# One PSUM bank a product in layer 2's input product, and raw weights stored in the step that joins them

## Chip, core and metric

The kernel runs on one core of a Trainium2 chip. The metric is the device time of one execution in microseconds (us). The core's engines run from queues of their own and wait for each other by semaphores: PE (TensorE, matrix products), DVE (VectorE), ACT (ScalarE), POOL (GpSimd) and SP, which issues the DMAs.

## The reference

Attention between 8 x 8 blocks of 512 tokens and 32 states, then two feed-forward layers. In float32:

```python
scores = scale * np.matmul(x, state.transpose(0, 1, 3, 2))       # 512 x 32 a head, softmax, then
xread = np.matmul(a, state)
sread = np.matmul(a2, x)                                         # a2: softmax of the transposed scores
x = concat([xread, sread])                                       # (8 * 544, 512)
gate = 1.0 / (1.0 + np.exp(-(x @ w_gate)))                       # layer 1, d_ff 1536
x = gate * (x @ w_val) @ w_out
h = x @ w_in                                                     # layer 2, d_ff 2048
g = np.where(h >= 1, h, np.where(h <= -1, 0.0, (h + 1) ** 2 / 4))
out = g @ w_out
```

## The kernel before

Each float32 product is made of three fast ones: both sides are split into a high and a low part (ACT copies the high part, DVE or POOL subtracts for the low one), and high x high, high x low and low x high are added in PSUM. The stages follow each other: attention and layer 1's gated product for the first four batches (`gated(0)`), its output product (`output1(0)`) mixed with the attention of the other four, `gated(1)`, `output1(1)`, layer 2's input product (`unit`, `unit_s`) and layer 2's output product (`second`). The order of the instructions on each engine is the order in which the code writes them.

**Layer 2's input product.** It is a two-by-two block product with seven products in place of eight (M1 to M7). Five blocks (0, 1, 2, "s", 3) follow each other, twice: a number is a pair of batches, "s" the states of all batches. A pair's block has four units, one for each 256 columns of weights; a unit runs the seven products in the order `PO` = M1, M6, M5, M7, M2, M3, M4, each of six matmuls of 512 columns, and calls `tick(n)` after each, where planned other work is written: loads and sums of the next block's operands (`load_y`, tiles `yr`, sums on POOL), their splits (`split_y`, tiles `yc`: high on ACT, low on POOL), the sums and splits of the second layer's output weights (`combos_w2`, tile `w2c`, on DVE and ACT), and stores of results (`puts`). M2 adds to the bank of M1, M3 to that of M5, M4 to that of M7. The unit takes its four banks as two tiles of two banks each from the pools `ps0` and `ps1` that all earlier stages use too:

```python
pa_, pb_ = ps_tile(0), ps_tile(1)
pm = {M1: pa_[:, 0], M6: pa_[:, 1], M5: pb_[:, 0], M7: pb_[:, 1]}
pm |= {M2: pm[M1], M4: pm[M7], M3: pm[M5]}
```

After M1, ACT copies its bank to `m1` (L977 of before); after M6, M5 and M7, DVE adds the bank to `m1` or `sg` (L947); then `act_g2` makes the activation: ACT's relu and square (L930, L931), which use a bank as scratch space, and DVE's clip (L932, the calls of `fins`). The last of a unit's activations are written after the next unit's first and second product (`later`).

**Raw weights.** In `output1(0)` the class `Weights` also converts the weights. One call of `slot` is a step: `high` takes the oldest joined tile, `join` (DVE, L166 and L172) makes the next tile `ca` from two halves, `parts` (ACT, L159 and L160) makes the halves of the one after, `load` loads another (`wraw`), and `flush` issues what is in `stores`. `ca` has three buffers. Weights of the kind "raw" (layer 2's output weights) are not split here: `high` only puts their store to `w2_dram` into `stores`, so it is issued in the step after the one that joined them.

Of the kernel before, what the change touches and what calls it, by code (L numbers as in the profile page):

```python
# [8 lines left out]
F32 = mybir.dt.float32  # L9
# [3 lines left out]
AF = mybir.ActivationFunctionType  # L13
ALU = mybir.AluOpType
AX = mybir.AxisListType
PSUM = bass.MemoryType.PSUM
# [9 lines left out]
def attention_moe_moe_kernel(  # L26
# [28 lines left out]
    nc = tc.nc  # L55
# [11 lines left out]
    NSB = B * N  # L67
# [4 lines left out]
    def pool(name, side="left", bufs=1, stack=None, **kw):  # L72
        return (stack or ctx).enter_context(
            tc.tile_pool(name=name, bufs=bufs, side=side, reuse_waits="tile", **kw)
        )

    st_ps = ExitStack()
# [4 lines left out]
    def ps_tile(k):  # L82
        return psets[k].tile([128, 2, 512], F32, tag="ps", name=f"ps{k}")
# [3 lines left out]
    half = work.tile([128, 1], F32, tag="half", name="half")  # L87
# [38 lines left out]
    def f32(ap):  # L126
        return ap.bitcast(F32)
# [5 lines left out]
    class Weights:  # L133
# [29 lines left out]
        def join(self):  # L163
            if self.first:
                r, a, y, dst = self.first.pop(0)
                nc.vector.scalar_tensor_tensor(  # L166
                    out=y, in0=r[:, 1::2], scalar=0x80000000, in1=y,
                    op0=ALU.bitwise_and, op1=ALU.bitwise_or,
                )
                part = getattr(dst, "kind", None) == "part"  # L170
                o, then = dst() if part else (a, None)
                nc.vector.scalar_tensor_tensor(  # L172
                    out=o, in0=a, scalar=3, in1=y,
                    op0=ALU.logical_shift_left, op1=ALU.bitwise_or,
                )
                if part:
                    then()
                else:
                    self.mid.append((a, dst))

        def high(self):
            if self.mid and getattr(self.mid[0][1], "kind", None) not in closed:
                a, dst = self.mid.pop(0)
                if getattr(dst, "kind", None) == "raw":
                    stores.append(lambda: nc.sync.dma_start(out=dst(), in_=f32(a)))
                    return
                hi, lo, then = dst()
                if len(hi.shape) == 3:
                    a = a.rearrange("p (k f) -> p k f", k=hi.shape[1])
                nc.scalar.activation(out=hi, in_=f32(a), func=AF.Copy)  # L190
                self.second.append((hi, lo, a, then))
# [24 lines left out]
    stores = []  # L216
# [5 lines left out]
    def mm3(ps, terms):  # L222
        n = len(terms)
        for i, (wh, wl, vh, vl) in enumerate(terms):
            nc.tensor.matmul(out=ps, lhsT=wh, rhs=vh, start=(i == 0), stop=False)
            nc.tensor.matmul(out=ps, lhsT=wh, rhs=vl, start=False, stop=False)
            nc.tensor.matmul(out=ps, lhsT=wl, rhs=vh, start=False, stop=(i == n - 1))
# [490 lines left out]
    M1, M2, M3, M4, M5, M6, M7 = range(7)  # L718
# [78 lines left out]
    def combos_w2(i):  # L797
# [27 lines left out]
        def store():  # L825
# [5 lines left out]
            load,  # L831
            [sum_(M5, M7, M1), sum_(M7, M3, M7), sum_(M6, M3, M5), sum_(M4, M2, M6)],
            high,
            [low(n) for n in (0, 2, 4, 6)],
            store,
# [91 lines left out]
    def act_g2(o, s, c):  # L927


        nc.scalar.activation(out=s, in_=c, func=AF.Relu, bias=half, scale=0.5)  # L930
        nc.scalar.activation(out=s, in_=s, func=AF.Square)  # L931
        return lambda: nc.vector.scalar_tensor_tensor(  # L932
            out=o, in0=s, scalar=1.0, in1=c, op0=ALU.min, op1=ALU.max
        )

    def store_g2(j, m, sg):
        return lambda: nc.sync.dma_start(out=hd_dram[j][:, 2 * m : 2 * m + 2], in_=sg)
# [3 lines left out]
    def late(n):  # L941
        while later and (n is None or later[0][0] <= n):
            later.pop(0)[1]()

    def unit(bp, m, tick):
        def add(o, a, b):
            nc.vector.tensor_tensor(out=o, in0=a, in1=b, op=ADD)  # L947

        w = w_t[m]
        pa_, pb_ = ps_tile(0), ps_tile(1)  # L950
        pm = {M1: pa_[:, 0], M6: pa_[:, 1], M5: pb_[:, 0], M7: pb_[:, 1]}
        pm |= {M2: pm[M1], M4: pm[M7], M3: pm[M5]}
        m1 = tmp.tile([128, 512], F32, tag="m1", name="m1", bufs=2)
        sg, fins = [None, None], {}

        def sg_tile(e):
            sg[e] = tmp.tile([128, 2, 512], F32, tag="sg", name="sg", bufs=4)

        def put(e):
            puts.append(store_g2(2 * bp + e, m, sg[e]))  # L960

        for n, j in enumerate(PO):
            y = yc_t[bp, j].rearrange("p l (k f) -> p l k f", k=2)
            more = j in (M2, M4, M3)
            for k in range(2):
                wh, wl = (w[:, l, WI[j], 128 * k : 128 * k + 128] for l in range(2))
                vh, vl = y[:, 0, k], y[:, 1, k]
                for i, (a, b) in enumerate(((wh, vh), (wh, vl), (wl, vh))):
                    nc.tensor.matmul(  # L969
                        out=pm[j], lhsT=a, rhs=b,  # L970
                        start=not more and k == 0 and i == 0,
                        stop=k == 1 and i == 2,
                        skip_group_check=more,
                    )
            late(n)
            if j == M1:
                nc.scalar.activation(out=m1, in_=pm[j], func=AF.Copy)  # L977
            elif j == M6:
                add(m1, pm[j], m1)
            elif j == M5:  # L980
                sg_tile(1)
                add(sg[1][:, 1], pm[j], m1)
            elif j == M7:
                add(sg[1][:, 1], pm[j], sg[1][:, 1])
            elif j == M2:
                sg_tile(0)
                fins[3] = act_g2(sg[1][:, 1], pm[M6], sg[1][:, 1])
            elif j == M3:
                s = spool.tile([128, 512], F32, tag="s", name="s", bufs=2)
                fins[0] = act_g2(sg[0][:, 0], s, pm[M1])  # L990
                fins[3]()
                add(sg[1][:, 0], pm[j], m1)
            elif j == M4:
                fins[0]()
                add(sg[0][:, 1], pm[j], m1)
                fins[1] = act_g2(sg[1][:, 0], pm[M5], sg[1][:, 0])
            tick(n)

        def last():
            fins[2] = act_g2(sg[0][:, 1], pm[M7], sg[0][:, 1])  # L1000
            fins[1]()
            put(1)

        later.append((0, last))
        later.append((1, lambda: (fins[2](), put(0))))

    def unit_s(m, tick):
        w = w_t[m]
        ps = ps_tile(0)[:, :, :NSB]
        bt = st_t["raw_c"].rearrange("p l (k f) -> p l k f", k=4)  # L1010
        dt = st_t["d_c"].rearrange("p l (k f) -> p l k f", k=4)
        for e in range(2):
            terms = ((M5, bt, 0), (M4, dt, 0)) if e else ((M1, bt, 0), (M2, bt, 2))
            mm3(
                ps[:, e],
                [
                    tuple(w[:, l, WI[j], 128 * k : 128 * k + 128] for l in range(2))
                    + (y[:, 0, o + k], y[:, 1, o + k])
                    for j, y, o in terms
                    for k in range(2)  # L1020
                ],
            )
            if e == 0:
                tick(0)
        late(None)
        sg = tmp.tile([128, 2, NSB], F32, tag="sg", name="sg", bufs=4)
        nc.scalar.activation(out=sg, in_=ps, func=AF.Relu, bias=half, scale=0.5)
        nc.scalar.activation(out=sg, in_=sg, func=AF.Square)
        nc.vector.scalar_tensor_tensor(
            out=sg, in0=sg, scalar=1.0, in1=ps, op0=ALU.min, op1=ALU.max  # L1030
        )
        tick(1)
        puts.append(store_g2(B, m, sg))

# [472 lines left out]


    st_o, st_m, st_c, st_x = ExitStack(), ExitStack(), ExitStack(), ExitStack()
    pm_ = pool("ycm", stack=st_m)  # L1510
    y_pools.update({i: pm_ for i in range(3, 10)})
    spool = pool("spool", stack=st_m)
# [101 lines left out]
    for p, b in blocks:  # L1614
        for mi in range(4):

            def tick(n):
                nonlocal t
                if puts and (b == "s" or n in (2, 4)):
                    puts.pop(0)()  # L1620
                for f in at.pop(t, ()):
                    f()
                t += 1
# [13 lines left out]

    st_m.close()
    st_e.close()
    st_ps.close()  # L1640
    hcps.append(pool("hcp1", stack=st_o))
    w2p = pool("w2b", stack=st_o, bufs=4)
    psp = pool("pso", stack=st_o, space=PSUM)
# [35 lines left out]
```

## Time and profile before

| | |
|---|---|
| median of 3 runs | 1749.75 us (1743.32 to 1749.83) |
| the profiled execution's own time | 1750.84 us |
| its span in the trace | 1749.1 us |
| PE busy | 1509.6 us, 86% |
| DVE, ACT, POOL busy | 972.7, 784.1, 225.8 us |
| matmuls of the input product (L969) | 1344, 389.9 us busy, 169.7 us idle before them |

Busy time is the time in which an engine has an instruction in work; a matmul that overlaps the next counts once. "Idle before" is the time an engine stood before the instructions of a group, and behind the arrow stands whose end released it. The times of the table's last rows and of all rows below are from one execution.

### The profile page before, as it was taken

Reading aid. Unit: us, or ns where it says so; the run is one execution under the profiler, and the core shown is the slowest. Engines: PE = TensorE matmul, PEld = TensorE weight load, DVE = VectorE, ACT = ScalarE, POOL = GpSimd, SP = SyncE. Lnnn points to the kernel's source line nnn. Section 1 sums busy time; section 2 is a strip of 40 time slices with the busy share of each in tenths; the row PEclk is TensorE's granted clock in tenths of the full one; section 3 lists DMA queues with packets and bytes.
Section 4 is the critical chain, followed back from the end, with each engine's and each line's share of the span. In section 5 each row is a group of like instructions: output and inputs, shape, how many; then the busy total and the mean of one; then the engine's idle time right before and its main releaser. Section 6 shows DMA issues by size and latency. Waiting matters only on the chain.

```text
span 1749.1 us, 29156 instructions
## 1 busy us (share of the span) xinstructions
PE 1509.6 (86%) x11984; PEld 1257.5 (72%) x11984; DVE 972.7 (56%) x1386; ACT 784.1 (45%) x1156; POOL 225.8 (13%) x108
## 2 busy tenths in 40 slices
PE   7999977899999999997776776767677799999997
PEld 6677756787677877985554564555555689999997
DVE  5766565644666266345343443444454468778775
ACT  6655365534654254233544445344354334443442
POOL 3000030000000000002332434234151000000000
PEclk9999999999999999999898988898889899999999
DMA  6245478745665499663233445523415674434432
GB/s 193 98 160 179 161 234 299 245 147 181 242 251 214 146 329 376 244 224 109 102 121 138 151 161 188 212 104 123 163 51 189 220 276 138 133 121 134 133 121 85
DMA packets 146453, 310.19 MB, mean 177 GB/s; under 512 B 15504, under 2 KB 82064, under 8 KB 143248
## 3 DMA queue, kind: packets, MB, share of 16 engines
q1 hardware_dynamic: 146056, 308.06, 50.4%
q8 instruction: 94, 1.54, 0.4%
q14 instruction: 39, 0.32, 0.1%
q10 hardware_dynamic: 264, 0.26, 0.1%
HBM read 187.17 MB, written 121.11 MB: 176 GB/s over the span
## 4 chain that ended last, share of the span: by engine, by line
PE 70%; ACT 12%; DVE 8%; DMA 6%; issue 4%; SPq 1%; POOL 0%; ACTq 0%; DVEq 0%
PE ps L969 17%; PE ps L524 15%; PE o L1042 6%; PE o L1040 6%; PE o L1041 6%; DVE sg L947 4%; ACT ps L930 4%; PE ps L641 4%; PE ps L640 4%; PE ps L642 4%; ACT ps L931 3%; PE ps L494 2%; DMA w_dram<-ca 2%; PE ps L302 1%; ACT s L930 1%
## 5 line engine op out<-in xcount | busy, mean ns | idle before, releaser
L969 PE MATMUL ps<-yc,wt 128*128 128x512 f32 x1344 | 389.9, 448 | 169.7 <-DVE sg L947 97.4
L969 PEld LDWEIGHTS ps<-yc,wt 128*128 128x128 f32 x1344 | 283.1, 217 | 275.4 <-DVE sg L947 125.7
L524 PE MATMUL ps<-at_hi,M 32*128 32x512 f32 x3072 | 261.2, 398 | 2.7 <-ACT e L326 1.4
L930 ACT ACTIVATE ps<-sg,half 128x512 f32<-128x512 f32 x96 | 66.5, 692 | 299.0 <-PE ps L969 190.3
L524 PEld LDWEIGHTS ps<-at_hi,M 32*128 32x128 f32 x3072 | 154.2, 183 | 46.5 <-issue 15.4
L641 PE MATMUL ps<-oh_lo,wo 128*128 128x512 f32 x368 | 148.9, 405 | 12.1 <-DVE oh_lo L609 12.1
L524 PE MATMUL ps<-at_lo,M 32*128 32x512 f32 x1536 | 158.5, 392 | 0.0
L640 PE MATMUL ps<-oh_hi,wo 128*128 128x512 f32 x368 | 152.4, 414 | 2.8 <-ACT oh_hi L607 2.8
L932 DVE SCALAR_TENSOR_TENSOR sg<-ps,sg 128x512 f32<-128x512 f32 x96 | 64.5, 687 | 154.6 <-ACT ps L931 85.2
L722 POOL TENSOR_TENSOR yr<-yr 128x1024 f32<-128x1024 f32 x28 | 66.5, 2392 | 640.5 <-DMA yr<-y_dram 611.9
L642 PE MATMUL ps<-oh_hi,wo 128*128 128x512 f32 x368 | 147.7, 401 | 0.0
L1040 PE MATMUL o<-wt,hc 128*128 128x256 f32 x476 | 136.1, 286 | 4.1 <-DVE sg L932 4.1
L1042 PE MATMUL o<-w,hc 128*128 128x256 f32 x476 | 136.2, 286 | 3.5 <-DVE hc L1088 3.5
L894 POOL TENSOR_TENSOR yc<-yr,yc 128x1024 fp32r<-128x1024 f32 x49 | 118.1, 2428 | 146.4 <-ACT yc L891 146.2
L1040 PE MATMUL o<-w,hc 128*128 128x256 f32 x476 | 136.0, 286 | 0.7 <-ACT hc L1084 0.7
L1041 PE MATMUL o<-wt,hc 128*128 128x256 f32 x476 | 135.9, 285 | 0.0
L1041 PE MATMUL o<-w,hc 128*128 128x256 f32 x476 | 135.9, 285 | 0.0
L1042 PE MATMUL o<-wt,hc 128*128 128x256 f32 x476 | 135.8, 285 | 0.0
L1084 ACT ACTIVATE hc<-hc 128x512 fp32r<-128x512 f32 (+1 forms) x108 | 65.1, 603 | 147.1 <-DMA hc<-hd_dram 144.1
L508 DVE TENSOR_TENSOR M<-ps,M 128x1024 fp32r<-128x1024 f32 x48 | 58.7, 1223 | 101.7 <-ACT M L502 101.7
L947 DVE TENSOR_TENSOR sg<-ps,m 128x512 f32<-128x512 f32 x96 | 66.0, 687 | 70.8 <-PE ps L969 70.7
L1084 ACT ACTIVATE hc<-hs 128x512 fp32r<-128x512 f32 (+1 forms) x144 | 80.0, 597 | 48.6 <-DVE hs L1081 48.6
(148 smaller groups left out, 2913.0 us busy)
## 6 DMA issues: line engine op xcount, KB each, us to landing
hd_dram<-sg SPq DMA_DIRECT2D x64, 512.0 KB, 3.3
h_dram<-sg SPq DMA_DIRECT2D x48, 512.0 KB, 4.6
oh_lo<-h_dram SPq DMA_DIRECT2D x48, 512.0 KB, 5.3
hc<-hd_dram SPq DMA_DIRECT2D x96, 256.0 KB, 4.0
yr<-y_dram SPq DMA_DIRECT2D x32, 512.0 KB, 7.5
wraw<-in_moe_w_out_dram SPq DMA_DIRECT2D x28, 512.0 KB, 4.3
w2c_dram<-w2c SPq DMA_DIRECT2D x8, 1792.0 KB, 5.9
wraw<-in_moe_w_gate_dram SPq DMA_DIRECT2D x48, 256.0 KB, 2.9
```

The source lines that it names most:

```text
L524: nc.tensor.matmul(out=ps[r // 2][:, r % 2], lhsT=M[o, l, e, c], rhs=a[o, e], start=(h == 0 and j == 0), stop=(h == H - 1 and j == 2),)
L640: nc.tensor.matmul(out=ps, lhsT=wh[:, c], rhs=hi, start=first, stop=False)
L641: nc.tensor.matmul(out=ps, lhsT=wh[:, c], rhs=lo, start=False, stop=False)
L642: nc.tensor.matmul(out=ps, lhsT=wl[:, c], rhs=hi, start=False, stop=last)
L894: low_on.tensor_tensor(out=t[:, 1, :n], in0=src, in1=f32(t[:, 0, :n]), op=SUB)
L930: nc.scalar.activation(out=s, in_=c, func=AF.Relu, bias=half, scale=0.5)
L947: nc.vector.tensor_tensor(out=o, in0=a, in1=b, op=ADD)
L969: nc.tensor.matmul(out=pm[j], lhsT=a, rhs=b, start=not more and k == 0 and i == 0, stop=k == 1 and i == 2, skip_group_check=more,)
L1040: nc.tensor.matmul(out=ps, lhsT=wh, rhs=vh, start=start and i == 0, stop=False)
L1041: nc.tensor.matmul(out=ps, lhsT=wh, rhs=vl, start=False, stop=False)
L1042: nc.tensor.matmul(out=ps, lhsT=wl, rhs=vh, start=False, stop=last)
L1084: nc.scalar.activation(out=get(j)[0], in_=raw(j), func=AF.Copy)
```

## The change

A new pool `psu` has four tags u0 to u3 of one bank and two buffers each, together the eight banks. It is opened at the start of layer 2's input product, where the pools `ps0` and `ps1` are now closed, and closed at its end. Each of a unit's four banks is a tile of its own, and `unit_s` takes two such tiles and runs the activation on each by itself. In `Weights`, `join` puts the store of a raw tile into `stores` in its own step, and `high` no longer sees raw tiles.

```diff
@@ class Weights, join and high
                 if part:
                     then()
+                elif getattr(dst, "kind", None) == "raw":
+                    stores.append(lambda: nc.sync.dma_start(out=dst(), in_=f32(a)))
                 else:
                     self.mid.append((a, dst))
 
         def high(self):
             if self.mid and getattr(self.mid[0][1], "kind", None) not in closed:
                 a, dst = self.mid.pop(0)
-                if getattr(dst, "kind", None) == "raw":
-                    stores.append(lambda: nc.sync.dma_start(out=dst(), in_=f32(a)))
-                    return
@@ unit
+    def u_bank(k):
+        return psu.tile([128, 512], F32, tag=f"u{k}", name=f"u{k}", bufs=2)
+
     def unit(bp, m, tick):
...
-        pa_, pb_ = ps_tile(0), ps_tile(1)
-        pm = {M1: pa_[:, 0], M6: pa_[:, 1], M5: pb_[:, 0], M7: pb_[:, 1]}
+        pm = {j: u_bank(k) for k, j in enumerate((M1, M6, M5, M7))}
         pm |= {M2: pm[M1], M4: pm[M7], M3: pm[M5]}
@@ unit_s
-        ps = ps_tile(0)[:, :, :NSB]
+        ps = [u_bank(e)[:, :NSB] for e in range(2)]
...
-                ps[:, e],
+                ps[e],
...
-        nc.scalar.activation(out=sg, in_=ps, func=AF.Relu, bias=half, scale=0.5)
-        nc.scalar.activation(out=sg, in_=sg, func=AF.Square)
-        nc.vector.scalar_tensor_tensor(
-            out=sg, in0=sg, scalar=1.0, in1=ps, op0=ALU.min, op1=ALU.max
-        )
+        for e in range(2):
+            act_g2(sg[:, e], sg[:, e], ps[e])()
@@ ahead of the input product, and behind it
+    st_ps.close()
+    psu = pool("psu", stack=st_m, space=PSUM)
...
-    st_ps.close()
```

On PE, this is the third unit of the first block before. yc0 to yc6 are the operands of M1, M6, M5, M7, M2, M3, M4, ps0 and ps1 the two tiles, wt the weights; a row stands for the product's six matmuls or, where its first one waits, for this one and the other five.

```order
L969 MATMUL ps0_10093<-yc0_9838,wt_9785 128x512 x6
L969 MATMUL ps0_10093<-yc1_9855,wt_9785 128x512 [waits Activation_49]
L969 MATMUL ps0_10093<-yc1_9855,wt_9785 128x512 x5
L969 MATMUL ps1_10094<-yc2_9879,wt_9785 128x512 x6
L969 MATMUL ps1_10094<-yc3_9929,wt_9785 128x512 [waits DVE_49]
L969 MATMUL ps1_10094<-yc3_9929,wt_9785 128x512 x5
L969 MATMUL ps0_10093<-yc4_9932,wt_9785 128x512 x6
L969 MATMUL ps1_10094<-yc5_9935,wt_9785 128x512 [waits DVE_49]
L969 MATMUL ps1_10094<-yc5_9935,wt_9785 128x512 x5
L969 MATMUL ps1_10094<-yc6_9938,wt_9785 128x512 [waits DVE_49]
L969 MATMUL ps1_10094<-yc6_9938,wt_9785 128x512 x5
```

The same unit after, with the tiles u0 to u3:

```order
L970 MATMUL u0_10102<-yc0_9838,wt_9785 128x512 x6
L970 MATMUL u1_10103<-yc1_9855,wt_9785 128x512 x6
L970 MATMUL u2_10104<-yc2_9879,wt_9785 128x512 x6
L970 MATMUL u3_10105<-yc3_9934,wt_9785 128x512 x6
L970 MATMUL u0_10102<-yc4_9937,wt_9785 128x512 [waits Activation_49]
L970 MATMUL u0_10102<-yc4_9937,wt_9785 128x512 x5
L970 MATMUL u2_10104<-yc5_9940,wt_9785 128x512 [waits DVE_49]
L970 MATMUL u2_10104<-yc5_9940,wt_9785 128x512 x5
L970 MATMUL u3_10105<-yc6_9943,wt_9785 128x512 [waits DVE_49]
L970 MATMUL u3_10105<-yc6_9943,wt_9785 128x512 x5
```

The matmuls and their order are the same. M6's wait for ACT now stands at M2, M7's wait for DVE is gone, and M3 and M4 still wait for DVE; which instruction of DVE or ACT it is, the name of the semaphore does not tell.

On SP, early in `output1(0)`, these are the DMAs around the first raw stores before (`w2_dram_0` and `w2_dram_1`; oh_lo, xr and xa are loads for the output product and the attention, DMAHW a DMA that came before).

```order
L150 DMA wraw_3845<-in_moe2_w_out_dram 128x1024 [waits DMAHW4_49,DVE_49,Activation_49]
L601 DMA oh_lo1_3878<-h_dram_0_100 128x2x512 [waits DMAHW5_49,PE_49]
L406 DMA xr_3880<-in_x_dram 128x4x256 [waits DMAHW6_49]
L150 DMA wraw_3888<-in_moe2_w_out_dram 128x1024 [waits DMAHW7_49,DVE_49]
L185 DMA w2_dram_0_126<-ca_3785 128x512 [waits DMAHW0_49]
L406 DMA xr_3924<-in_x_dram 128x4x256 [waits DMAHW1_49,PE_49]
```

The same stretch after:

```order
L150 DMA wraw_3845<-in_moe2_w_out_dram 128x1024 [waits DMAHW4_49,DVE_49,Activation_49]
L179 DMA w2_dram_0_126<-ca_3785 128x512 [waits DMAHW5_49,DVE_49]
L600 DMA oh_lo1_3879<-h_dram_0_100 128x2x512 [waits DMAHW6_49,PE_49]
L405 DMA xr_3881<-in_x_dram 128x4x256 [waits DMAHW7_49]
L150 DMA wraw_3889<-in_moe2_w_out_dram 128x1024 [waits DMAHW0_49,DVE_49]
L179 DMA w2_dram_1_127<-ca_3841 128x512 [waits DMAHW1_49,DVE_49]
L405 DMA xr_3925<-in_x_dram 128x4x256 [waits DMAHW2_49,PE_49]
```

Each raw store has moved up by one step, to the place right behind the step's load of `wraw`, and waits for DVE there. On DVE, ACT, PE and POOL the order of `output1(0)` is the same as before.

## Rows read from the trace of the kernel before

**Rows 1.** The page: busy us and share, then busy tenths in 40 slices.

```profile
PE 1509.6 (86%) x11984; PEld 1257.5 (72%) x11984; DVE 972.7 (56%) x1386; ACT 784.1 (45%) x1156; POOL 225.8 (13%) x108
...
PE   7999977899999999997776776767677799999997
```

**Rows 2.** Three stretches: their length, busy us by engine, PEclk, DMA share, GB/s.

```profile
450.00:600.00 150.00, 148.77 (x2302) 115.45 (x2300) 82.06 (x94) 71.91 (x95) 0.00 (x0) 1.00 0.56 204
...
798.00:1384.00 586.00, 415.63 (x1545) 308.86 (x1543) 255.27 (x374) 258.65 (x374) 194.11 (x83) 0.88 0.40 144
```

**Rows 3.** Groups of 798 to 1384 us: busy us, mean ns | idle before.

```profile
L969 PE MATMUL ps<-yc,wt 128*128 128x512 f32 x1344 | 389.9, 448 | 169.7 <-DVE sg L947 97.4 <-ACT m L977 69.3 <-DVE sg L1029 3.0
```

**Rows 4.** Timeline of PE in the second block: start, us taken.

```profile
945.24 3.01 PE L969 MATMUL ps<-yc,wt 128*128 128x512 f32 x12 [1.68 <-ACT m L977]
949.04 4.38 PE L969 MATMUL ps<-yc,wt 128*128 128x512 f32 x18 [0.78 <-DVE sg L947]
955.50 4.46 PE L969 MATMUL ps<-yc,wt 128*128 128x512 f32 x12 [2.08 <-DVE sg L947]
961.36 3.00 PE L969 MATMUL ps<-yc,wt 128*128 128x512 f32 x12 [1.40 <-ACT m L977]
```

**Rows 5.** Groups of 798 to 1384 us on DVE, ACT and POOL.

```profile
L894 POOL TENSOR_TENSOR yc<-yr,yc 128x1024 fp32r<-128x1024 f32 x49 | 118.1, 2428 | 146.4 <-ACT yc L891 146.2
...
L947 DVE TENSOR_TENSOR sg<-ps,m 128x512 f32<-128x512 f32 x96 | 66.0, 687 | 70.8 <-PE ps L969 70.7
L930 ACT ACTIVATE ps<-sg,half 128x512 f32<-128x512 f32 x95 | 65.8, 692 | 299.0 <-PE ps L969 190.3 <-DVE sg L947 107.8
...
L931 ACT ACTIVATE ps<-ps 128x512 f32<-128x512 f32 x94 | 54.7, 582 | 3.0
L891 ACT ACTIVATE yc<-yr 128x1024 fp32r<-128x1024 f32 x53 | 54.1, 1054 | 11.4 <-PE ps L969 10.6 <-DMA hd_dram<-sg 0.4 <-PE ps L642 0.3
...
L977 ACT ACTIVATE m<-ps 128x512 f32<-128x512 f32 x32 | 18.9, 592 | 1.3 <-PE ps L969 1.3
L817 ACT ACTIVATE w2c<-w2c 128x1792 fp32r<-128x1792 f32 x8 | 13.6, 1701 | 8.8 <-DVE w2c L722 8.8
```

**Rows 6.** DVE's sums of w2c: one group, then line 722 (min/median/max ns).

```profile
L722 DVE TENSOR_TENSOR w2c<-w2c 128x256 f32<-128x256 f32 x32 | 24.4, 771 | 0.1
...
L722 DVE TENSOR_TENSOR w2c<-w2c x64: 410/680/2862, 820.7 to 1311.9; 128x256 f32<-128x256 f32 x32, 128x512 fp32r<-128x512 f32 x24, 128x256 fp32r<-128x256 f32 x8
```

**Rows 7.** Timeline of PE in a state block: first and last of 48 matmuls.

```profile
1007.85 0.28 PE L225 MATMUL ps<-yc,wt 128*128 128x256 f32 x1
...
1013.48 0.28 PE L227 MATMUL ps<-yc,wt 128*128 128x256 f32 x1
```

**Rows 8.** Waits of 215 to 400 us: total us, times, longest.

```profile
ACT ca L159 <- DMA w_dram<-ca: 34.3, 13, 7.3
...
PE ps L287 <- ACT ev L647: 7.1, 1, 7.1
...
PE ps L346 <- ACT ev L647: 3.3, 1, 3.3
```

**Rows 9.** Timeline of SP and ACT in 284 to 300 us (w_dram is `w2_dram`).

```profile
286.92 0.42 SPq L185 DMA_DIRECT2D w_dram<-ca  x1
...
291.45 0.42 SPq L185 DMA_DIRECT2D w_dram<-ca  x1
...
297.79 0.66 ACT L159 ACTIVATE ca<-wraw 128x512 f32<-128x512 f32 x1 [3.14 <-DMA w_dram<-ca]
```

**Rows 10.** Chain of what ended last, 1380 to 1420 us: start, us.

```profile
1386.52 1.30 DVE sg L932 x2
1396.71 14.68 DMA hc<-hd_dram
```

**Rows 11.** DMA issues of 798 to 1384 us: KB each, median us to landing.

```profile
yr<-y_dram SPq DMA_DIRECT2D x28, 512.0 KB, 7.3
```

## The prediction, made before the run

> **What bounds the kernel now.** I read the page first. TensorE (PE) is busy 86% of the span, and the digits of its row are not evenly spread: they stand at 7 to 9 before slice 18, at 6 and 7 from slice 18 to slice 31 (counted from 0), and at 9 after that [rows 1]. Slices 18 to 31 are layer 2's input product. Cut by stages [rows 2], this stage (798 to 1384 us) has PE busy for 415.6 of 586 us at a granted clock of 0.88, while a dense stage (450 to 600 us) has 148.8 of 150 us at 1.00. No other engine is near its limit in it: VectorE (DVE) 255 us, ScalarE (ACT) 259 us, GpSimd (POOL) 194 us, DMA share 0.40. So the stage is not bound by an engine's work but by PE's waits, and the groups of the stage say which: the 1344 product matmuls are busy 389.9 us and stand idle 169.7 us before them, of which 97.4 us end with a DVE addition at L947 and 69.3 us with ACT's copy at L977 [rows 3].
>
> The timeline of one unit shows where [rows 4]. A unit is seven products M1, M6, M5, M7, M2, M3, M4 of six matmuls each. PE runs M6 and M5 (x12), stops 0.78 us until M5's addition has ended, runs M7, M2, M3 (x18), stops 2.08 us until M3's addition has ended, runs M4 and the next unit's M1 (x12), stops 1.40 us until M1's copy has ended. From M6 to M6 that is 961.36 - 945.24 = 16.1 us. None of the three products that stop needs the result it waits for: M7 and M5, M4 and M3, M1 and M6 go to different banks, but each pair shares one two-bank tile, and the order of before shows the wait at the tile.
>
> **The change, part by part.**
>
> *One tile for each bank.* In the order of after, M6 and M7 have no wait left. M2 waits for ACT (M1's copy), M3 and M4 for DVE (the additions of M5 and M7): these are true, since M2, M3, M4 add to the banks of M1, M5, M7. The question is whether they come in time.
>
> Floor first. Six more matmuls in a run cost 4.38 - 3.01 = 1.37 us [rows 4], so 0.228 us for one; I take 0.23, 42 x 0.23 = 9.66 us for a unit and 1.38 us a product.
>
> Then the chain, counted from a unit's first matmul, with 0.33 us from a product's nominal end to its reader (a run of twelve takes 3.01 us, 0.27 more than 12 x 0.228; I round up) and 0.05 us a handover. M7's product is readable at 4 x 1.38 + 0.33 = 5.85; its addition (0.69) ends at 6.54. ACT then does four pairs of relu and square and the next unit's copy. Relu and square on M6's bank end at 7.9 (0.69 and 0.58), those on M1's product at 9.25, when DVE has done M3's addition; those on M5's bank at 10.6; M4's addition, readable at 7 x 1.38 + 0.33 = 9.99, ends by 10.8; those on M7's bank at 12.15; the copy (0.59) at 12.75 (durations from [rows 5]). The next unit's M2 starts at 9.66 + 4 x 1.38 = 15.2: 2.4 us of slack. M5's addition ends by 14.8, and the next M3 wants it at 16.55; M7's addition ends at 16.2, and M4 wants it at 17.9: 1.7 us of slack each. So a plain unit would run with no stop, at 9.66 us.
>
> Work of the others in the same time: a block of four units has ACT at 4 x 5.9 + 7 operand splits of 1.05 + about one 1.7 us split of w2c (8 over 32 units, so 1 in 4) = 32.7 us of 38.6; POOL at 11 x 2.43 = 26.7 us [rows 5]. DVE: 255 of some 350 us. All fit, none with much room.
>
> What I add to the floor. DVE's sums for the second weights (w2c, L722, 64 of them) read two SBUF tiles; alone one takes 0.41 us (128x256), but the mean of these is 0.77 and the longest of all 2.86 us [rows 6]. The 32 of the first form cost 24.4 us where 32 x 0.41 = 13.1 would do; the same for all 64 is some 22 us of stretching, at a POOL share of 194/586 = 0.33. In a stage of 350 us POOL's share is 0.55, and the same stretching grows to 22 x 0.55 / 0.33 = 37 us. What one costs over the 1.7 us of slack lands on PE, so I take a little under half, 17 us. ACT's split of w2c waited 8.8 us in all for those sums; I take 3 of it. Together 20 us, bounds 0 and 37 + 9 = 46.
>
> The Trainium skill (SBUF — State Buffer, section "Who interferes with whom") says why: a DVE instruction with two SBUF inputs and a GpSimd instruction that reads SBUF exclude each other, and the later one waits for the whole of the earlier. By that rule each of the 64 would meet a running POOL operation with chance 0.55 and wait for half of 2.43 us on average: 64 x 0.55 x 1.2 = 42 us of DVE time against the 37 above. The longest row, 2.86 us, about one POOL operation and its own time, agrees.
>
> The sum for the 32 units: busy plus idle before is 389.9 + 169.7 = 559.6 us; after, 32 x 9.66 = 309 + 20 = 329. Gain 230 us, from 559.6 - 309 = 250 down to 559.6 - 355 = 204. The lower clock is in this: a run of x12 took 4.46 us after a wait where others took 3.01 [rows 4], and the busy 389.9 us exceed the floor by 81 us for this and for restarts.
>
> *The state blocks* (two of four small units each): the 48 matmuls of 256 columns from 1007.85 to 1013.48 us take 5.6 us [rows 7], two units' worth. Two relu, square and clip chains on 256 columns replace one on 512, at most some 1 us more of ACT and of DVE a unit, under 2.8 us of matmuls. I put this at 0.
>
> *Raw weights stored in the step that joins them.* Before, the store of a `ca` tile was issued one step after its join: the one issued at 291.45 could have gone with the step of 286.92, and ACT stood 3.14 us until it had landed, at 297.8, since `ca` has three buffers [rows 9]. ACT waited so 13 times, 34.3 us; PE felt it where an evacuation (L647) was queued on ACT behind the wait, 7.1 and 3.3 us [rows 8]. Issued one step earlier (4.5 us there), a store lands before ACT asks (wait of 3.14). New: on SP the store waits for the join, and the loads of `oh_lo`, `xr` and `xa` queue behind it; but the `wraw` load just ahead of it waits for the same join's first half already, so SP stands some 0.7 us longer. I take 8 us of the 10.4, bounds 0 and 12.
>
> *The end of the stage.* The last clips (1386.52 to 1387.8 us) still precede the last stores, and the output product then waits for a load of hc issued at 1396.71 that took 14.68 us [rows 10]. First output matmuls may start some 4 us sooner, and then wait that much longer: 0.
>
> **Sum.** The profiled execution took 1750.84 us (span 1749.1), 1.1 above the median of 1749.75. 1750.84 - 230 - 8 = 1512.8; on the median's footing 1512.
>
> **Rivals.**
> *The other engines become the bound.* If each w2c operation meets a whole POOL operation, DVE gets 64 x (2.43 - 0.5) = 123 us more than bare, about 100 over today's 255: 355 us, above PE's 309 + 23. With its handovers exposed the stage is near 400 us: 586 - 400 = 186, less 8: 1557 us. For it: 2.86 us has occurred. Against: the mean is 0.77, and half the time POOL is idle.
> *Loads come late.* The yr loads took 7.3 us to land [rows 11], and the stage's DMA share would go from 0.40 to 0.67. If they take 12, POOL's eleven operations start 5 us later in each of eight blocks and the last split is 1 to 4 us late for PE: 8 to 32 us, so 1520 to 1545.
> *The clock falls instead of rising (slower).* If the dense stage ran at 1.2 GHz, half of the other level, a matmul would cost up to twice 0.23 us, a unit 19.3 us, 32 of them 618 against 559.6: 1751 + 58 - 8 = 1801. It decides only if more than eight in ten matmuls run slow (9.66 x (1 + share) above today's 559.6 / 32 = 17.5). Against: 1.00 was granted in 450 to 600 us at 99% busy, 0.88 only where PE waits [rows 2]. The Trainium skill (TensorE: Matmul & The Clock Gate, Part 1) has activity release the throttle, which agrees.
> *The waits stay.* If the products still stop, at M2, M3 and M4, for chains that move along, only the second edit gains: 1742 us. Against: the slack of 1.7 to 2.4 us above.
>
> **How the numbers follow.** Forecast 0.78, engines bound 0.10, late loads 0.07, waits stay 0.03, clock 0.02. The forecast alone spans 1750.8 - 250 - 12 = 1489 to 1750.8 - 204 = 1547. The range takes in the late loads and most of the first rival: 1488 to 1558. Half a per cent (9 us) is about what can be told from no change: faster 0.95, same 0.03 (waits stay at their worst), slower 0.02.
>
> **What would show it.** Right: the product matmuls' idle time under 30 us, the stage near 350 us at a clock of 0.97 or more, M6 and M7 with no idle before them, ACT's waits on the raw stores near 0. Wrong: idle before M2 (ACT's copy) or M3 and M4 of over 1 us in most units; w2c means above 1.5 us; POOL or ACT waiting for yr loads in each block.

## The result, and the profile after

The change takes 1508.62 us (median of 4 runs, 1503.97 to 1517.75) against 1747.44 us of before, run beside it: ratio 0.8642, 95% interval 0.8596 to 0.8687. The profiled execution took 1503.97 us with a span of 1501.9 us; all rows of after are from it.

The page of after, PE's busy time and its row of 40 slices. The 6s and 7s of slices 18 to 31 [rows 1] are gone:

```profile
PE 1422.1 (95%) x11984; PEld 1214.1 (81%) x11984; DVE 1002.0 (67%) x1394; ACT 781.6 (52%) x1172; POOL 233.0 (16%) x108
...
PE   7999989999999999999999999989998999999997
```

The stage in one window, from its first product to its last (columns as in [rows 2]), and the same cut of before, which is 1.4 us less than the 586 us of [rows 2]:

```profile
776.70:1137.60 360.90, 338.26 (x1539) 274.69 (x1538) 283.61 (x381) 256.17 (x389) 201.25 (x83) 1.00 0.64 232
```

```profile
798.50:1383.10 584.60, 414.43 (x1539) 307.96 (x1538) 254.58 (x373) 258.16 (x372) 194.11 (x83) 0.88 0.40 144
```

It is 360.9 us long where it was 584.6, at a granted clock of 1.00 instead of 0.88. It starts 21.8 us earlier (776.7 against 798.5 us). The span shrank by 1749.1 - 1501.9 = 247.2 us: 223.7 in the stage, 21.8 before it, and 1.7 behind it. The medians differ by less, 238.8 us, since before's profiled execution lies 3.4 us above its median and after's 4.65 below. Some 2 to 3.5 of the 21.8 us arise at the start, where the kernels are alike: the granted clock of the first 60 us was 0.86 in before's execution and 0.91 in this one of after. In after's execution of experiment 8 it was 0.86 too, and the stage starts at 781.4 us, 17.1 earlier than in before.

Groups of the stage (busy, mean ns | idle before). The first answers to [rows 3], the others to [rows 5, 6]:

```profile
L970 PE MATMUL u<-yc,wt 128*128 128x512 f32 x1344 | 314.8, 393 | 19.5 <-DVE sg L949 9.4 <-ACT m L978 8.0 <-DVE sg L931 2.1
...
L721 DVE TENSOR_TENSOR w2c<-w2c 128x256 f32<-128x256 f32 (+1 forms) x64 | 84.4, 1333 | 11.6 <-DMA w2c<-w_dram 10.9 <-ACT w2c L816 0.5
...
L929 ACT ACTIVATE u<-sg,half 128x512 f32<-128x512 f32 x95 | 65.5, 690 | 84.9 <-DVE sg L949 83.6
...
L890 ACT ACTIVATE yc<-yr 128x1024 fp32r<-128x1024 f32 x53 | 54.2, 1056 | 9.9 <-POOL yr L721 9.2 <-PE ps L641 0.3
...
L816 ACT ACTIVATE w2c<-w2c 128x1792 fp32r<-128x1792 f32 x8 | 13.6, 1704 | 4.6 <-DVE w2c L721 4.6
```

The product matmuls stand idle 19.5 us instead of 169.7. ACT's relu waited 190.3 us for PE before; now all but 1.3 of its 84.9 us end with a DVE addition, as the sums it needs do.

PE's timeline from M2 of the stage's third unit on, where [rows 4] had three stops in each unit:

```profile
802.50 10.06 PE L970 MATMUL u<-yc,wt 128*128 128x512 f32 x42 [0.41 <-ACT m L978]
813.55 3.27 PE L970 MATMUL u<-yc,wt 128*128 128x512 f32 x12 [0.99 <-ACT m L978]
817.85 35.82 PE L970 MATMUL u<-yc,wt 128*128 128x512 f32 x156 [1.04 <-DVE sg L949]
854.19 42.02 PE L970 MATMUL u<-yc,wt 128*128 128x512 f32 x183 [0.52 <-ACT m L978]
```

The last row is more than four units without a stop, 183 matmuls in 42.02 us, 0.230 us each: the floor of the prediction.

### The profile page after: what moved, and what is told of

Same layout as the page of the kernel before. It is cut to its first block, busy times and chain, and to the rows that moved or that the text cites. A ratio compares the mean times of both kernels' runs of the same rounds, so it can differ in the third digit from the quotient of the medians.

```text
span 1501.9 us, 29195 instructions
## 1 busy us (share of the span) xinstructions
PE 1422.1 (95%) x11984; PEld 1214.1 (81%) x11984; DVE 1002.0 (67%) x1394; ACT 781.6 (52%) x1172; POOL 233.0 (16%) x108
## 5 line engine op out<-in xcount | busy, mean ns | idle before, releaser
L970 PE MATMUL u<-yc,wt 128*128 128x512 f32 x1344 | 314.8, 393 | 19.5 <-DVE sg L949 9.4
L970 PEld LDWEIGHTS u<-yc,wt 128*128 128x128 f32 x1344 | 251.1, 189 | 82.4 <-DVE sg L949 16.5
L639 PE MATMUL ps<-oh_hi,wo 128*128 128x512 f32 x368 | 150.7, 409 | 3.0 <-ACT oh_hi L606 3.0
L641 PE MATMUL ps<-oh_hi,wo 128*128 128x512 f32 x368 | 145.9, 397 | 0.0
L893 POOL TENSOR_TENSOR yc<-yr,yc 128x1024 fp32r<-128x1024 f32 x49 | 122.4, 2526 | 6.7 <-ACT yc L890 6.4
L929 ACT ACTIVATE u<-sg,half 128x512 f32<-128x512 f32 x96 | 66.2, 690 | 85.0 <-DVE sg L949 83.6
L501 ACT ACTIVATE M<-ps 128x1024 fp32r<-128x1024 f32 x48 | 49.2, 1026 | 102.9 <-PE ps L493 102.8
L608 DVE TENSOR_TENSOR oh_lo<-oh_lo,oh_hi 128x1024 fp32r<-128x1024 f32 x48 | 58.6, 1222 | 55.8 <-ACT oh_hi L606 52.2
```

What stands on the lines that cost most here:

```text
L639: nc.tensor.matmul(out=ps, lhsT=wh[:, c], rhs=hi, start=first, stop=False)
L641: nc.tensor.matmul(out=ps, lhsT=wl[:, c], rhs=hi, start=False, stop=last)
L893: low_on.tensor_tensor(out=t[:, 1, :n], in0=src, in1=f32(t[:, 0, :n]), op=SUB)
L970: nc.tensor.matmul(out=pm[j], lhsT=a, rhs=b, start=not more and k == 0 and i == 0, stop=k == 1 and i == 2, skip_group_check=more,)
```

## The experiments

Ratios are to the kernel before, run beside the others on the same chip (medians of 1746.0, 1746.4 and 1747.5 us). Four kernels put one pair of banks back into one tile; the table has the stage of each, with before and after, from windows like those above, idle being the length less PE's busy time.

| kernel | time, us | stage, us | PE busy | PE idle | clock |
|---|---|---|---|---|---|
| before | 1747.44 | 584.6 | 414.4 | 170.2 | 0.88 |
| M5 and M7 share a tile | 1645.16 | 498.1 | 382.5 | 115.6 | 0.92 |
| the same, scratch moved | 1586.02 | 439.7 | 362.5 | 77.2 | 0.96 |
| M1 and M6 share a tile | 1626.44 | 479.2 | 391.0 | 88.2 | 0.88 |
| the same, scratch moved | 1602.33 | 455.5 | 372.6 | 82.9 | 0.90 |
| after | 1508.62 | 360.9 | 338.3 | 22.6 | 1.00 |

**1. The raw stores alone.** Before, with this part of the change:

```diff
+                elif getattr(dst, "kind", None) == "raw":
+                    stores.append(lambda: nc.sync.dma_start(out=dst(), in_=f32(a)))
...
-                if getattr(dst, "kind", None) == "raw":
-                    stores.append(lambda: nc.sync.dma_start(out=dst(), in_=f32(a)))
-                    return
```

> The kernel before with the second edit alone: a raw tile's store goes into the queue in the step that joins it; the two-bank tiles stay. Theory A: the 18 us that the trace of after gained between 250 and 372 us come from ACT's waits for the landed stores alone: four stops of PE behind ACT (7.1, 1.5, 1.8 and 3.3 us before) shrink to under 2 us together, and the granted clock of the stretch goes from 0.93 to 1.00, which takes some 6 us from the matmuls' busy time. Time about 1729 us (18 less). Rival: only the two stops behind the evacuation are the edit's, as the prediction summed it, and the rest is scatter between executions: about 1739 us (8 less). Layer 2's input product stays at about 585 us in both.

Measured: 1731.04 us (10 runs), ratio 0.9909 (0.988 to 0.9938), so 16 us less by the ratio, with 10 to 21 in the interval (the medians differ by 15). Theory A holds; the 8 us of the prediction lie outside.

**2. The banks alone.** After, with the raw stores back in `high`, where before had them:

```diff
-                elif getattr(dst, "kind", None) == "raw":
-                    stores.append(lambda: nc.sync.dma_start(out=dst(), in_=f32(a)))
...
+                if getattr(dst, "kind", None) == "raw":
+                    stores.append(lambda: nc.sync.dma_start(out=dst(), in_=f32(a)))
+                    return
```

> The changed kernel without the second edit: one-bank tiles in layer 2's input product, raw stores one step after the join as before. Theory A: the two edits lie in different stages and add: about 1747 - 224 = 1524 us, the input product at about 361 us, ACT's waits on the raw stores back at some 34 us in 13 waits. Rival: with the raw stores late the earlier stage gives less or more than its own 18 us, because what it delays is caught up later: then the time is outside 1517 to 1533 us.

Measured: 1524.13 us, ratio 0.8745 (0.87 to 0.8791). The two edits add: 16 us and 222 (1746.0 less 1524.13).

**3. M5 and M7 in one tile of two banks.**

```diff
+    def u_pair():
+        return psu.tile([128, 2, 512], F32, tag="up", name="up", bufs=2)
...
-        pm = {j: u_bank(k) for k, j in enumerate((M1, M6, M5, M7))}
+        up = u_pair()
+        pm = {M1: u_bank(0), M6: u_bank(1), M5: up[:, 0], M7: up[:, 1]}
```

> The changed kernel with M1 and M6 on tiles of one bank, M5 and M7 again on one tile of two banks. Theory A (a chain of hand-overs, walked with the rows' durations): M7 stops for M5's addition 0.8 us, as before. M4 stops for M3's addition, but shorter than the 2.08 us before, since ACT's first relu no longer waits for M2's product, so DVE's clip ahead of M3's addition is early: about 0.8 us. With two restarts of 0.3 us a unit of 11.8 us, 378 us for 32, 44 more than after: about 1553 us. Rival B (each stop is worth what it was before): the 97.4 us that ended with DVE's additions stay, with their restarts and the lower clock: 1610 to 1640 us.

Measured: 1645.16 us, ratio 0.9445 (0.9387 to 0.9502). My theory fell, and the rival was nearer though still too fast. PE's timeline of it, from M7 of one unit to M7 of the next (u is a tile of one bank, up the shared one):

```profile
905.12 2.58 PE L974 MATMUL up<-yc,wt 128*128 128x512 f32 x6 [2.17 <-DVE sg L952]
907.50 2.20 PE L974 MATMUL u<-yc,wt 128*128 128x512 f32 x6
909.54 1.52 PE L974 MATMUL up<-yc,wt 128*128 128x512 f32 x6
911.84 1.67 PE L974 MATMUL up<-yc,wt 128*128 128x512 f32 x6 [0.78 <-DVE sg L952]
913.35 2.91 PE L974 MATMUL u<-yc,wt 128*128 128x512 f32 x12
916.10 1.52 PE L974 MATMUL up<-yc,wt 128*128 128x512 f32 x6
920.01 1.65 PE L974 MATMUL up<-yc,wt 128*128 128x512 f32 x6 [2.39 <-DVE sg L952]
```

M4 stops 0.78 us (911.84), but M7 stops 2.17 and 2.39 us, not the 0.78 that before had at this place [rows 4]. ACT's timeline has the reason:

```profile
914.28 0.69 ACT L929 ACTIVATE up<-sg,half 128x512 f32<-128x512 f32 x1 [3.19 <-DVE sg L952]
...
916.84 0.59 ACT L982 ACTIVATE m<-u 128x512 f32<-128x512 f32 x1
```

This relu needs only M3's sum, in SBUF; it writes to M5's bank, as scratch, and so to the shared tile, which M4's addition still reads: ACT stands 3.19 us. The copy of the next unit's M1 comes late behind it, and with it M5's addition and M7.

**4. M1 and M6 in one tile instead**, with the same `u_pair`; `unit_s` takes the banks that are left:

```diff
-        pm = {j: u_bank(k) for k, j in enumerate((M1, M6, M5, M7))}
+        up = u_pair()
+        pm = {M1: up[:, 0], M6: up[:, 1], M5: u_bank(2), M7: u_bank(3)}
...
-        ps = [u_bank(e)[:, :NSB] for e in range(2)]
+        ps = [u_bank(2 + e)[:, :NSB] for e in range(2)]
```

> The changed kernel with M5 and M7 on tiles of one bank, M1 and M6 again on one tile of two banks. Theory A (the chain): M6 stops for M1's copy, which stands on ACT behind the last relu and square of the unit before, about 2.0 us with 0.3 us of restart; M7 and M4 do not stop. A unit of 11.9 us, 381 us for 32, 47 more than after: about 1556 us. Rival B (each stop is worth what it was before): 69.3 us that ended with ACT's copy stay, with the lower clock behind them: 1580 to 1610 us. If A holds for this and for the run with the other pair, the two false waits are not additive: either one alone gone gives some four fifths of the gain.

Measured: 1626.44 us, ratio 0.9331 (0.9282 to 0.938); slower than both theories. In its groups, ACT's relu on M6's bank waits 158.7 us for PE, for M2's product in the other bank of the tile, whose value it does not use:

```profile
L974 PE MATMUL up<-yc,wt 128*128 128x512 f32 x576 | 179.1, 454 | 85.5 <-ACT m L982 85.5
...
L929 ACT ACTIVATE up<-sg,half 128x512 f32<-128x512 f32 x32 | 22.2, 693 | 171.7 <-PE up L974 158.7 <-DVE sg L952 13.0
```

So against before, freeing M1 and M6 saves 584.6 - 498.1 = 86.5 us, freeing M5 and M7 saves 105.4, and both together 223.7: the parts make up 192 of it, they nearly add. The other 32 are what the pairs cost together or what the new pool does besides; no run separates these, since none had both pairs shared in it. I had expected either alone to give some four fifths.

**5. Experiment 3 with the scratch elsewhere.** ACT's scratch for M5's and M7's activations goes to the banks of M6 and M1:

```diff
-                fins[1] = act_g2(sg[1][:, 0], pm[M5], sg[1][:, 0])
+                fins[1] = act_g2(sg[1][:, 0], pm[M6], sg[1][:, 0])
...
-            fins[2] = act_g2(sg[0][:, 1], pm[M7], sg[0][:, 1])
+            fins[2] = act_g2(sg[0][:, 1], pm[M1], sg[0][:, 1])
```

> This is the kernel with M5 and M7 in one tile of two banks (1645 us, stage 498 us, 109 us of stops behind DVE's additions), with ACT's scratch for the activations of M5's and M7's sums moved to the banks of M6 and M1, which are tiles of their own. Theory A: what made that kernel miss its expectation is that ACT's relu, which only uses M5's bank as scratch, waits for M4's addition because it shares a tile with it, and so the whole unit's activations, m1's copy and M5's addition come late. Then relu no longer waits, M7's stop falls from 2.2 to 2.4 us a unit to what the wait for M5's addition itself is, 0.8 to 1.0 us, M4's stays near 0.8 us, the stops fall from 109 to 50 to 65 us and the granted clock rises from 0.92, and the time to 1565 to 1595 us. Rival B: the additions are late by themselves and the pair's two waits cost what they cost: 1630 to 1650 us, M7's stops at 2 us and more.

Measured: 1586.02 us, ratio 0.9072 (0.9045 to 0.9098), 59 us less than experiment 3, inside theory A's range. PE's timeline:

```profile
908.20 1.66 PE L974 MATMUL up<-yc,wt 128*128 128x512 f32 x6 [0.78 <-DVE sg L952]
...
914.74 1.66 PE L974 MATMUL up<-yc,wt 128*128 128x512 f32 x6 [0.79 <-DVE sg L952]
```

Here M4 and M7 stop 0.78 and 0.79 us. Over the whole stage the stops fell from 112.6 to 76.0 us in 64, not to the 50 to 65 that theory A had, since some are longer:

```profile
PE up L974 <- DVE sg L952: 76.0, 64, 3.9
```

What the shared tile still costs is the 439.7 - 360.9 = 79 us to after; what it cost by the scratch is the 58 us above that.

**6. Experiment 4 with the scratch elsewhere.** The activation on M6's bank takes a tile in SBUF as scratch:

```diff
-                fins[3] = act_g2(sg[1][:, 1], pm[M6], sg[1][:, 1])
+                s3 = spool.tile([128, 512], F32, tag="s", name="s", bufs=2)
+                fins[3] = act_g2(sg[1][:, 1], s3, sg[1][:, 1])
```

> This is the kernel with M1 and M6 in one tile of two banks (1626 us, stage 479 us, 85.5 us of stops behind m1's copy), with ACT's scratch for the activation on M6's sum moved from M6's bank to an SBUF tile. Theory A: relu waited 158.7 us there for M2's product, whose bank it shares a tile with and doesn't use; without that the m1 copy is no longer late, M6's stop falls from 2.4 to 2.7 us a unit to 1.0 to 1.4 us (the copy's 0.59 us and its handovers), and the time falls by 38 to 55 us and by what the granted clock (0.88) gives back, to 1545 to 1590 us. Rival B: the stop at M6 is the copy itself and the clock stays low as in the kernel before: 1610 us or more.

Measured: 1602.33 us, ratio 0.9167 (0.9136 to 0.9198), 24 us less, between the two theories. Eleven of M6's 32 stops take 1.27 us, as theory A has it, but others take up to 7.61, and all together are 80.2 us, hardly less than the 85.5 of experiment 4. DVE's timeline ahead of the longest, at 1047.27 us, shows what I had not counted:

```profile
1033.51 2.23 DVE L721 TENSOR_TENSOR w2c<-w2c 128x256 f32<-128x256 f32 x1
1035.66 0.68 DVE L952 TENSOR_TENSOR sg<-u,sg 128x512 f32<-128x512 f32 x1
1036.26 4.55 DVE L721 TENSOR_TENSOR w2c<-w2c 128x256 f32<-128x256 f32 x2
1040.73 2.82 DVE L931 SCALAR_TENSOR_TENSOR sg<-s,sg 128x512 f32<-128x512 f32 x1
```

Three of w2c's sums (0.41 us each where nothing holds them up) take 6.8 us, and the clip behind them 2.82. This clip now has both inputs in SBUF and is stretched as w2c's sums are: the median of the 32 is 0.69 us, the longest 2.89. Its group against that of a clip with one input in PSUM, where none takes over 0.69:

```profile
L931 DVE SCALAR_TENSOR_TENSOR sg<-s,sg 128x512 f32<-128x512 f32 x32 | 35.0, 1093 | 28.9 <-ACT s L930 28.9
...
L931 DVE SCALAR_TENSOR_TENSOR sg<-s,up 128x512 f32<-128x512 f32 x32 | 21.8, 682 | 2.7 <-ACT s L930 2.7
```

So this kernel moved one wait and brought another. That ACT's false wait was all of experiment 4's miss is not shown.

**7. The ca buffer.** Before, with the raw stores as late as they were, but a fourth buffer for every fourth tile `ca`:

```diff
-                a = conv.tile([128, 512], U32, tag="ca", name="ca", bufs=CB[1])
+                self.n += 1
+                if self.alt and getattr(dst, "kind", None) == "raw" and self.n % 4 == 0:
+                    a = self.alt.tile([128, 512], U32, tag="ca4", name="ca", bufs=1)
+                else:
+                    a = conv.tile([128, 512], U32, tag="ca", name="ca", bufs=CB[1])
...
+    weights.alt = pool("alt", stack=st_s)
```

> The kernel before, with the raw stores one step late as they were, but every fourth raw tile in a fourth buffer, so that a tile is written again one step later. Theory A (ACT's wait for the buffer is the whole of the second edit's gain): the wait falls as it did in after, and the time is that of the second edit alone, some 18 us less than before, about 1729 us. Rival (it is the store's earlier place on SP and in the DMA queues, ahead of the loads, that helps): no gain, 1742 to 1750 us.

Measured: 1727.18 us, ratio 0.9892 (0.984 to 0.9943): the gain of the raw stores, 19 us here and 16 in experiment 1, without moving a store. ACT's waits for a raw store from 215 to 400 us are 9.0 us in it, 11.4 in experiment 1 and 34.3 in before. The same buffer in after:

> The changed kernel with every fourth raw tile in a fourth buffer. ACT still waited 12.1 us in 6 waits for raw stores in after. Theory A: PE's stops behind ACT are nearly gone already (under 2.5 us in that stretch), so the waits vanish and the time does not move: within 3 us of the changed kernel run in the same call. Rival: the 12 us of ACT waits still delay PE, 5 to 10 us less.

Measured: 1508.78 us, ratio 0.8645 (0.8588 to 0.8703), no change within the scatter: its four runs (1506.22 to 1515.69) overlap those of after in experiment 8. ACT no longer waits for a raw store there. So ACT's wait for a buffer is the whole of the raw stores' gain, as far as these runs tell, and nothing of it is left.

**8. After, once more**, beside experiment 9:

> The changed kernel as it is, on the chip of the three other kernels of this call, to compare them with: 1504 to 1518 us, as measured before.

Measured: 1511.59 us, ratio 0.865 (0.8606 to 0.8694), the stage 363.8 us.

**9. w2c on POOL.** After, with the 64 sums and low parts of w2c on POOL:

```diff
-            return lambda: tt(nc.vector, raw(o), raw(p), raw(q))
+            return lambda: tt(nc.gpsimd, raw(o), raw(p), raw(q))
...
-                nc.vector, box[0][:, 1, n:m], raw(n, m), f32(box[0])[:, 0, n:m]
+                nc.gpsimd, box[0][:, 1, n:m], raw(n, m), f32(box[0])[:, 0, n:m]
```

> The changed kernel with the 64 sums and low parts of w2c on POOL in place of DVE. Theory A (what is left above the floor in the input product is DVE standing behind POOL in these sums, mean 1.33 us for work of some 0.5): DVE loses 84 us of busy time, all in the stage, PE's idle time before the product matmuls falls from 19.5 to under 10 us and the time by 8 to 15 us, to about 1497 us. POOL rises from 194 to about 255 us of 350. Rival C: POOL, in whose queue these sums now stand between the sums and low parts of the next block's operands, becomes late, ACT and PE wait for it: 1510 to 1540 us.

Measured: 1515.79 us, ratio 0.868 (0.8635 to 0.8724), 4 us more than experiment 8; theory A fell, rival C holds. From its waits in the stage:

```profile
ACT w2c L816 <- POOL w2c L721: 27.4, 5, 10.5
...
PE u L970 <- ACT m L978: 17.9, 5, 5.8
PE u L970 <- DVE sg L931: 6.9, 1, 6.9
PE u L970 <- DVE sg L949: 2.6, 3, 1.6
```

The stops behind DVE's additions fell from 9.4 to 2.6 us, so w2c on DVE had been their cause for the most part. In their place ACT's split waits for POOL's sums, and the copies queued behind it are late for M2.

**10. Only the low parts on POOL**, the second of the two edits above alone:

> The changed kernel with only the 32 low parts of w2c on POOL in place of DVE; the 32 sums, for which ACT's split waits, stay on DVE. Theory A: the stops that end with DVE (9.4 us before the product matmuls) come from w2c operations held up by POOL, and about half of those go, while ACT's w2c split waits for DVE as before (5 us); the stage falls by 3 to 8 us, the time to 1500 to 1506 us. Rival B: POOL, with 32 operations of some 1.5 us more, makes its yc low parts late as it did with all 64 operations (1516 us): 1510 to 1520 us.

Measured: 1517.37 us (6 runs), ratio 0.8674 (0.8651 to 0.8697); theory A fell. ACT's wait for w2c did go down, to 2.8 us, but the idle time before the products is 26.1 us, not less:

```profile
L970 PE MATMUL u<-yc,wt 128*128 128x512 f32 x1344 | 318.3, 397 | 26.1 <-DVE sg L949 16.4 <-ACT m L978 6.9 <-DVE sg L931 2.1
```

DVE waited 19.5 us for w2c's loads (10.9 in after), and ACT's operand splits 14.8 us for POOL (9.2). Which of them made the stops longer is not settled, and of the 16.5 us in the two spans 8 lie ahead of the stage, where the kernels are alike. Neither experiment 9 nor 10 was faster than after.

## Why the prediction was right, and where a term was not

**The units.** 559.6 us of busy and idle time became 314.8 + 19.5 = 334.3, a gain of 225.3 where I had 230. The floor was right to the digit (0.230 us a matmul). The residual was 19.5 idle and 5.8 us of busy time over the floor, together 25 for the 20 I added. M2, M3 and M4 kept their waits and nearly always met them: PE stopped 19 times (9 for DVE's additions, 9 for the copy, 1 for a clip), for at most 2.2 us; M6 and M7 never did.

**That the pairs shared a tile was the cause** is shown: giving one pair its shared tile back brings the stops back (3, 4), and with the scratch out of the way M7 and M4 stop for 0.78 us where nothing else is late (5), as long as M7 did in before. My chain counted only PE's false waits. ACT's scratch writes to the shared tile were a good part of it (59 us between 3 and 5, for this pair); the change takes both away, so the sum didn't need them, but my expectations for 3 and 4 did and missed.

**The residual's mechanism.** w2c on DVE took 84.4 us against 53 before; at bare durations (40 forms of 0.41 and 24 of 0.68 us) it is 33, so the stretching is 52 us, where I had 37. The longest operation was 2.90 us, the mean 1.33, under the 1.5 at which I would have been wrong. The view of DVE with one of the longest stops, M4's of 2.18 us at 983.93:

```profile
979.34 0.69 DVE L949 TENSOR_TENSOR sg<-u,m 128x512 f32<-128x512 f32 x1 [2.85 <-DMA hd_dram<-sg]
981.91 1.36 DVE L721 TENSOR_TENSOR w2c<-w2c 128x256 f32<-128x256 f32 x1 [1.89 <-DMA w2c<-w_dram]
983.20 0.68 DVE L949 TENSOR_TENSOR sg<-u,sg 128x512 f32<-128x512 f32 x1
```

Two more causes stand in it that I had not priced: DVE waits for a store that must free `sg` (2.85 us), then, with M7's addition queued behind, for w2c's load (1.89 us; 10.9 in the stage). How much of the stops is stretching and how much such waits was not separated. I had w2c costing 17 us at M3 and M4; the stops behind DVE's additions are 9.4 us, and 8.0 are at M2 behind ACT's copy. The next rows of DVE, ACT and PE lead to such a stop:

```profile
983.80 4.55 DVE L721 TENSOR_TENSOR w2c<-w2c 128x256 f32<-128x256 f32 x2
...
989.58 0.69 ACT L929 ACTIVATE u<-sg,half 128x512 f32<-128x512 f32 x1 [3.04 <-DVE sg L949]
...
992.65 1.67 PE L970 MATMUL u<-yc,wt 128*128 128x512 f32 x6 [1.63 <-ACT m L978]
```

M3's addition is queued behind two sums of w2c that take 4.55 us; ACT's relu waits 3.04 us for it, and the copy, queued behind two pairs of relu and square, ends too late for M2. Seven of the nine stops at M2 come about in this way, with two operations of w2c of together 3.0 to 5.0 us, or one behind its load, ahead of M3's addition; ahead of the other two ACT's own splits stand. My chain gave the copy 2.4 us of slack and put what w2c costs at M3 and M4 alone, so nearly half of the idle time came by a path that it leaves out. Experiment 9 shows that the stops behind DVE's additions go with w2c; those behind the copy grew there by another wait, so for them the cause is read from the timelines and not tested.

The Trainium skill (SBUF — State Buffer, "Who interferes with whom") has DVE instructions with two SBUF inputs contend with GpSimd's reads, and those with one not. Experiment 6 agrees: the clip took 1.09 us on average with its scratch in SBUF, and in the same stage 0.68 with one input in PSUM. The estimate by that section of the Trainium skill, 42 us of stretching, was nearer to the 52 measured than mine.

**The raw stores** are the term that was mis-sized: "I take 8 us of the 10.4, bounds 0 and 12" against 16 (10 to 21). The mechanism held: ACT's waits for a raw store, and what PE waited for, from 215 to 400 us in after:

```profile
ACT ca L159 <- DMA w_dram<-ca: 12.1, 6, 2.7
```

```profile
PE ps L286 <- ACT ev L646: 1.5, 1, 1.5
...
PE ps L345 <- ACT ev L646: 0.4, 1, 0.4
...
PE ps L394 <- ACT e L377: 0.3, 1, 0.3
...
PE ps L420 <- ACT u L396: 0.2, 1, 0.2
```

34.3 us are 12.1, the two stops of 7.1 and 3.3 us [rows 8] are 1.5 and 0.4. "Waits near 0" was too much. What I left out stands in the same list of before, stops behind ACT's e and u, on the same engine as the wait:

```profile
PE ps L421 <- ACT u L397: 2.0, 2, 1.8
...
PE ps L395 <- ACT e L378: 1.5, 1, 1.5
```

They are 0.2 (u) and 0.3 us (e) after; with the raw stores late again in experiment 2 they are 1.9 and 2.5. That makes 7.1 + 3.3 + 2.0 + 1.5 = 13.9 us of stops, of which 2.4 stay. The rest is clock. The same 97 DVE operations, 797 matmuls before and 795 after, span these windows:

```profile
250.00:373.00 123.00, 105.09 (x797) 86.18 (x796) 73.90 (x97) 64.50 (x87) 3.10 (x2) 0.93 0.73 248
```

```profile
247.00:352.00 105.00, 98.60 (x795) 80.82 (x795) 73.63 (x97) 64.02 (x87) 3.03 (x2) 1.00 0.82 289
```

18 us in all: 11.5 of idle time (17.9 to 6.4) and 6.5 of busy time, at a granted clock of 1.00 instead of 0.93. I had priced two of the stops, and not the slower matmuls behind them.

**The edits at nothing.** The state blocks and what else lies between the units are 360.9 - 334.3 = 26.6 us against 584.6 - 559.6 = 25.0, so 1.6 us more where I had 0: PE stops 3.2 us in the state blocks behind clips, 0.5 before. The end of the stage, by the chain that ended last: the first output product comes 0.7 us after the last clip's start, and a load of hc is awaited longer than before [rows 10]:

```profile
1139.68 0.70 DVE sg L931
1140.42 0.39 PE o L1038
...
1147.73 17.15 DMA hc<-hd_dram
```

The stretch behind the stage is 1.7 us shorter, near the 0 predicted.

**The rivals.** DVE is busy 283.6 of 360.9 us, no bound. The loads of yr landed in 8.1 us (median of the stage's 28, 7.3 in before), not 12, and ACT waited 9.2 us for POOL in all, so late loads are a small part. The clock rose to 1.00. The lower clock I counted into the gain (81 us of busy time above the floor before) came back nearly whole: 389.9 - 314.8 = 75.

That the time, 1508.6, is within 4 us of the forecast is partly luck: two misses cancel. By the runs the banks gave 222 us (experiment 2) where the sum has 230, and the raw stores 16 where it has 8.

## What to carry to other kernels

Where independent PSUM banks are parts of one tile, ask of each wait, PE's and those of every engine that uses a bank of the tile, scratch writes too, whether the instruction needs the very result that ended it: a false wait on ACT came back on PE as a late copy. Price a stop on PE with the slower matmuls that follow it, and list everything that queues behind the waiting instruction, not only the longest stops. DVE's sums with two SBUF inputs grew beside a busier POOL (w2c from 53 to 84 us), and moving them to POOL moved the wait too.

## What was not expected of the hardware

The stops cost from about half to four fifths as much again in slower matmuls: against after, M5 and M7 in one tile give PE 93 us more of idle time and 44 more of busy time, M1 and M6 66 and 53. With M1 and M6 in one tile PE idles less than with M5 and M7 in one (88.2 against 115.6 us) but is busy 8.5 us longer, at 0.88 against 0.92. Its timeline shows where:

```profile
908.39 2.93 PE L974 MATMUL up<-yc,wt 128*128 128x512 f32 x6 [2.42 <-ACT m L982]
```

The six matmuls behind the stop take 2.93 us, about twice 6 x 0.23: the granted clock from 908.39 to 911.12 us is 0.50, the lower of its two levels (1.2 GHz). In experiment 6 six behind a stop took 1.66, at 1.00:

```profile
902.85 1.66 PE L974 MATMUL up<-yc,wt 128*128 128x512 f32 x6 [1.27 <-ACT m L982]
```

But in experiment 3 six took 2.58 us behind a stop of 2.17 (clock 0.58) and 1.65 behind one of 2.39 (clock 1.00), so the length of the one stop alone does not decide it; what does is left open.
